# Second stage in 6 chunks of 384 tokens instead of 8 of 288, and the two attention products of a unit issued together

## The chip, the cores and the metric

The kernel runs on one core of a Trainium2 chip. The time is the device time of one execution in microseconds (us). Engines are named as in the profile: PE is TensorE (PEld its weight loads), DVE is VectorE, ACT is ScalarE, POOL is GpSimd, SP is SyncE, which issues the DMAs. "Lnnn" is a line of the kernel before.

## The reference

Inputs are q, k, v of shape (4, 8, 576, 64): batch, heads, sequence, head dimension. Three layers follow each other.

```python
# 1 attention, per head: a pooled one over means of 4 positions, and a local one
out_d = softmax(q_d @ k_d.T / 8) @ v_d          # 144 x 144, repeated 4 times along the sequence
out_local = softmax(where(abs(i - j) < 4, q @ k.T / 8, -1e9)) @ v
x = (repeat(out_d, 4) + out_local)              # to (4, 576, 512)
# 2 channel MLP on the layer norm
x = x + maximum(layernorm(x) * g_ln @ w_ch1, 0) @ w_ch2        # 512 -> 2048 -> 512
# 3 second MLP on mixes of each token with the one ahead of it
xk = mu_k * x + (1 - mu_k) * x_prev ; xr = mu_r * x + (1 - mu_r) * x_prev
k = maximum(xk @ w_k, 0)                                       # 512 -> 1024
out = sigmoid(xr @ w_r) * (k * k @ w_v)                        # 1024 -> 512
```

## The kernel before

All activations lie with the features on the partitions and the tokens along the row. The 2304 tokens are cut into 8 chunks of 288 (N, half a sequence). Weights come as float64 and are turned into float32 by ACT and DVE, then into a high and a low float32r part; a product of two float32 matrices is three float32r matmuls (`mm3`, L192 to L194): high by high, high by low, low by high.

**First stage** (the loop over `seq`): for each chunk c and each f of 16 hidden blocks, `emit_l1` multiplies the normed chunk with a block of the first weight (12 matmuls of 128x288 into h_ps), `emit_l2` multiplies the block's result with the second weight (12 matmuls into four accumulators acc). Between them run the attention and the layer norm of the next chunk, written as generators. A `slot` comes after every six large matmuls; it feeds a budget of DVE time to the generators, and a generator that yields GAP stops until the next feed. So GAP puts at least one feed, six large matmuls, between two steps. `emit_x2` adds the result to x and writes it to memory (x2d, one tensor per chunk); its last token is also copied to edge.

**A unit** of the attention (`unit`) is one chunk and one pair of heads: 8 x 4 units. Its products on PE are the scores (L269 in windows of 30 keys, L273 pooled), four transposes (L316, tile tp), the windowed weights by v (L325, six products) and the pooled weights by the pooled values vd (L333, four products). L325 and L333 write parts of the same tile av; tp and av share one bank of PSUM. Plain float32 products are issued as two matmuls each in the trace, so L325 counts 12 and L333 counts 8 per unit there. Between L325 and L333 stands a GAP:

```python
        yield GAP
        for t in range(2):
            for h in range(2):
                nc.tensor.matmul(
                    av[64 * h:64 * h + 64, N:N + QD],
                    vd[:, t, 64 * h:64 * h + 64], PdT[:, 2 * h + t, :],
```

**Second stage** (the loop over c behind the comment "phase B"): per chunk 8 groups of 12 matmuls with w_k, 4 groups of 12 with w_r and 4 groups of 24 with w_v, 240 in all, each group into one of eight banks (b_ps). `mix` makes xk and xr of a chunk on ACT and DVE, from x2in, which `load_x2` fetches from x2d two chunks ahead; the token ahead of the chunk comes from edge. `start_b`, during the last chunk of the first stage, closes the pools of the attention, opens those of the second stage, and starts `load_b` (the weights, tile wf) and the first mix. Program order on each engine is set by the tile framework's scheduler, which moves an instruction ahead where its inputs and its buffer are ready.

Of the kernel before, what the change touches and what calls it, by code (L numbers as in the profile page):

```python
# [22 lines left out]
N = S // 2  # L23
# [6 lines left out]
NK = DK // 128  # L30


@with_exitstack
def tile_block(ctx: ExitStack, tc: tile.TileContext, qT, kT, vw, vr, vec, mask, w1, w2, wk, wv, wr, out):
# [17 lines left out]
    mask_t = const.tile([128, 2, 3, WIN], F32, name="mask_t")  # L52
    edge = const.tile([128, NCH, KT, 1], F32, name="edge")
    x2d = [dram.tile([128, KT, N], F32, name=f"x2d{c}") for c in range(NCH)]
# [5 lines left out]
    pln = actx.enter_context(tc.tile_pool(name="pln", bufs=1))  # L60

# [142 lines left out]
    PTs = [const.tile([128, 6, 4, 24], F32, name=f"PT{i}") for i in range(2)]  # L204
    kz = [const.tile([128, 2, S + 6], F32, name=f"kz{i}") for i in range(2)]
    kdz = [const.tile([128, 2, SD], F32, name=f"kdz{i}") for i in range(NHP)]
    Ps = [const.tile([128, 6, 32], F32, name=f"P{i}") for i in range(2)]
# [26 lines left out]
    def unit(c, hp, nxt):  # L234
# [95 lines left out]
        yield GAP  # L330
# [32 lines left out]
    def over_features(ps, a, parts):  # L363
        """the mean over the 128 partitions, on all of them"""
# [148 lines left out]
    def emit_x2(c):  # L513
# [6 lines left out]
        nc.gpsimd.tensor_copy(edge[:, c], x[:, :, N - 1:N])  # L520
        nc.sync.dma_start(x2d[c], x)
# [64 lines left out]
    # phase A  # L586
# [29 lines left out]
    def start_b():  # L616
# [3 lines left out]
        xk.extend(bp.tile([128, KT, N], F32R, name=f"xk{i}") for i in range(2))  # L620
# [3 lines left out]
    def load_x2(c):  # L624
        t = xp.tile([128, KT, N + 1], F32, tag="x", name="x2in")
        nc.sync.dma_start(t[:, :, 1:N + 1], x2d[c])
        if c % 2 == 0:
            nc.gpsimd.memset(t[:, :, 0:1], 0.0)
        else:
            nc.gpsimd.tensor_copy(t[:, :, 0:1], edge[:, c - 1])  # L630
        x2in[c] = t

    def mix(c, which):
# [3 lines left out]
        for k in range(KT + 1):  # L637
            if k > 0:
                nc.scalar.copy(dh[:, k - 1, :], prev)
            if k < KT:  # L640
                a = late["bp"].tile([128, N], F32, tag="mixa", name="mixa", bufs=3)
                nc.scalar.activation(a, t[:, k, 1:N + 1], AF.Copy, scale=vec_t[:, 1 + which, k:k + 1])  # L642
# [3 lines left out]
            if k < KT:  # L646
                nc.vector.scalar_tensor_tensor(a, t[:, k, 0:N], omu[:, which, k:k + 1], a, op0=ALU.mult, op1=ALU.add)
# [27 lines left out]
    # phase B  # L675
    bp = late["bp"]
    k2 = [[wpool.tile([128, 4, N], F32R, tag="w", name="k2") for _ in range(2)] for _ in range(2)]
    xr.extend(wpool.tile([128, KT, N], F32R, tag="w", name="xr") for _ in range(2))
# [16 lines left out]
    for c in range(NCH):  # L695
        for f in range(NK):
# [6 lines left out]
            nc.scalar.activation(r, ps[:, 0:N], AF.Relu)  # L703
            nc.vector.tensor_tensor(r, r, ps[:, 0:N], op=ALU.mult)
# [6 lines left out]
        nxt = Feeder(mix(c + 1, 0)) if c + 1 < NCH else Feeder(iter(()))  # L711
        rs = []
        for o in range(KT):
# [3 lines left out]
            for k in range(KT):  # L717
                mm3(ps[:, 0:N], wh[:, k, s], wl[:, k, s], xr[0][:, k, :], xr[1][:, k, :], k == 0, k == KT - 1)
            e = bp.tile([128, N], F32, tag=f"e{o}", name="e")
            nc.vector.tensor_scalar(e, ps[:, 0:N], -87.0, None, op0=ALU.max)  # L720
# [5 lines left out]
        for o in range(KT):  # L726
            ps = bank()
            s = slice(128 * o, 128 * o + 128)
            for f in range(NK):
                (wh, wl), (kh, kl), i = WV[f // 4], k2[f // 4], f % 4  # L730
                mm3(ps[:, 0:N], wh[:, i, s], wl[:, i, s], kh[:, i, :], kl[:, i, :], f == 0, f == NK - 1)
            nxt.feed(2.0)
            ot = bp.tile([128, N], F32, tag="ot", name="ot", bufs=2)
            nc.vector.tensor_tensor(ot, rs[o], ps[:, 0:N], op=ALU.mult)
            nc.sync.dma_start(out[128 * o:128 * o + 128, N * c:N * c + N], ot)
        nxt.drain()
        if c + 1 < NCH:
            pending = Feeder(mix(c + 1, 1))
        if c + 2 < NCH:
# [71 lines left out]
```

## Time and profile before

| | |
|---|---|
| runs | 813.71, 812.79, 815.49 us; median 813.71 us |
| profiled execution | span 812.2 us from the first to the last instruction; the page has no other time of it |
| busy share of the span | PE 95%, PEld 90%, DVE 68%, ACT 51%, POOL 10% |
| instructions | PE 6630, DVE 1330, ACT 1067, POOL 133 |
| moved by DMA | 76.12 MB, 94 GB/s over the span |
| granted PE clock | 0.985 of full speed over the span |

The share of PE is an average over a start in which weights are converted, the first stage and the second stage. A matmul's entry in the timeline is longer than the distance to the next start, because matmuls overlap in the array; the distance of two starts is what a matmul costs. Entries of equal instructions that follow each other closely stand in one row with their count (x12).

### The profile page before, as it was taken

The numbers are of one execution on the slowest core, as the hardware profiler recorded it, in microseconds if no ns is written. First come the engines' busy times: TensorE is split into PE (matmuls) and PEld (weight loads), VectorE is DVE, ScalarE is ACT, GpSimd is POOL, SyncE is SP. The second block draws the span as 40 slices with busy tenths as digits, with TensorE's granted clock in tenths as the row PEclk, the third lists the DMA queues.
The fourth block names the chain that finished last, engine by engine and source line by source line (L and its number), as shares of the span: only waits on it lengthen the run. The fifth ranks groups of instructions, "written<-read, shape, count | busy, mean of one in ns | idle before, by whom it ended". The sixth has DMA issues, their size and how long they took to land.

```text
span 812.2 us, 16778 instructions
## 1 busy us (share of the span) xinstructions
PE 771.0 (95%) x6630; PEld 734.9 (90%) x6630; DVE 554.7 (68%) x1330; ACT 410.7 (51%) x1067; POOL 78.7 (10%) x133
## 2 busy tenths in 40 slices
PE   2559989999999999999999999999999999999998
PEld 1349979999999999999999999999999999999998
DVE  5989987656656645665756545736886976967855
ACT  4889965544544543543554543735454453453440
POOL 3210331001122001122001001001000000000000
PEclk9859999999999999999999999999999999999999
DMA  7797542332342331442332210522202101010000
GB/s 208 232 316 236 152 141 80 110 100 81 98 148 90 104 102 53 115 150 76 100 110 78 91 55 9 158 74 89 59 1 60 51 9 59 20 40 31 8 23 30
DMA packets 39182, 76.12 MB, mean 94 GB/s; under 512 B 4672, under 2 KB 23232, under 8 KB 39104
## 3 DMA queue, kind: packets, MB, share of 16 engines
q1 hardware_dynamic: 39104, 75.06, 29.3%
q8 instruction: 52, 0.85, 0.5%
q14 instruction: 26, 0.21, 0.1%
HBM read 60.36 MB, written 14.68 MB: 92 GB/s over the span
## 4 chain that ended last, share of the span: by engine, by line
PE 90%; DVE 5%; ACT 2%; DMA 2%; issue 1%; SPq 0%; ACTq 0%
PE b_ps L192 10%; PE b_ps L193 10%; PE b_ps L194 10%; PE h_ps L192 9%; PE acc L192 9%; PE h_ps L193 8%; PE acc L194 8%; PE acc L193 8%; PE h_ps L194 8%; PE sc L273 2%; PE av L325 2%; PE sc L269 2%; DMA raw<-in_w 1%; PE av L333 1%; DVE raw L77 1%; PE tp L316 1%
## 5 line engine op out<-in xcount | busy, mean ns | idle before, releaser
L499 DVE SCALAR_TENSOR_TENSOR hl<-h_ps,hh 128x288 fp32r<-128x288 f32 x128 | 58.0, 454 | 86.8 <-ACT hh L498 86.1
L498 ACT ACTIVATE hh<-h_ps 128x288 fp32r<-128x288 f32 x128 | 51.8, 405 | 78.1 <-PE h_ps L194 77.6
L192 PE MATMUL b_ps<-k,wbh 128*128 128x288 f32 x256 | 75.8, 296 | 0.0
L193 PE MATMUL b_ps<-xk,wbh 128*128 128x288 f32 x256 | 75.5, 295 | 0.0
L193 PE MATMUL b_ps<-k,wbh 128*128 128x288 f32 x256 | 75.5, 295 | 0.0
L194 PE MATMUL b_ps<-xk,wbl 128*128 128x288 f32 x256 | 75.5, 295 | 0.0
L194 PE MATMUL b_ps<-k,wbl 128*128 128x288 f32 x256 | 75.3, 294 | 0.0
L192 PE MATMUL b_ps<-xk,wbh 128*128 128x288 f32 x256 | 75.1, 293 | 0.0
L723 DVE RECIPROCAL e<-e 128x288 f32<-128x288 f32 x32 | 62.1, 1944 | 0.1
L305 ACT COPY PT<-T 32x144 f32<-32x144 f32 x128 | 39.5, 309 | 29.7 <-DVE T L301 28.4
L519 POOL TENSOR_TENSOR x<-x2t,x 128x288 f32<-128x288 f32 x32 | 25.0, 813 | 300.5 <-DVE x2t L518 300.5
L642 ACT ACTIVATE mixa<-x2in,vec_t 128x288 f32<-128x288 f32 x64 | 31.6, 530 | 38.3 <-DVE xr L645 36.0
L194 PEld LDWEIGHTS b_ps<-k,wbl 128*128 128x128 f32 x256 | 48.2, 188 | 0.0
L192 PEld LDWEIGHTS b_ps<-xk,wbh 128*128 128x128 f32 x256 | 48.1, 188 | 0.0
L193 PEld LDWEIGHTS b_ps<-xk,wbh 128*128 128x128 f32 x256 | 48.1, 188 | 0.0
L194 PEld LDWEIGHTS b_ps<-xk,wbl 128*128 128x128 f32 x256 | 48.1, 188 | 0.0
L193 PEld LDWEIGHTS b_ps<-k,wbh 128*128 128x128 f32 x256 | 48.1, 188 | 0.0
L192 PEld LDWEIGHTS b_ps<-k,wbh 128*128 128x128 f32 x256 | 48.0, 187 | 0.0
L77 DVE SCALAR_TENSOR_TENSOR raw<-rm 128x512 uint32<-128x512 uint32 x52 | 37.0, 715 | 13.1 <-ACT rm L76 12.7
L693 DVE TENSOR_TENSOR k<-kr,k 128x288 fp32r<-128x288 f32 x64 | 29.2, 457 | 23.6 <-ACT k L692 23.5
L703 ACT ACTIVATE kr<-b_ps 128x288 f32<-128x288 f32 x64 | 26.2, 410 | 36.2 <-PE b_ps L194 36.1
L76 ACT ACTIVATE rm<-raw 128x512 uint8<-128x512 uint8 x52 | 39.9, 784 | 7.7 <-DVE rm L73 7.2
(162 smaller groups left out, 2608.4 us busy)
## 6 DMA issues: line engine op xcount, KB each, us to landing
raw<-in_w SPq DMA_DIRECT2D x32, 512.0 KB
v<-in_vw SPq DMA_DIRECT2D x32, 192.0 KB
bd<-raw SPq DMA_DIRECT2D x20, 256.0 KB
wf<-bd SPq DMA_DIRECT2D x10, 512.0 KB
q<-in_qT SPq DMA_DIRECT2D x32, 148.0 KB
kz<-in_kT SPq DMA_DIRECT2D x32, 145.5 KB
r<-in_vr SPq DMA_DIRECT2D x32, 144.0 KB
x2d<-x SPq DMA_DIRECT2D x8, 576.0 KB
```

What stands on the lines that cost most here:

```text
L76: nc.scalar.activation(low, top, AF.Copy, scale=1.0 / 32.0, bias=-31.0 / 64.0)
L77: nc.vector.scalar_tensor_tensor(raw[:, 0:512].bitcast(U32), ru, 3, m, op0=ALU.logical_shift_left, op1=ALU.bitwise_or)
L192: nc.tensor.matmul(ps, wh, ah, start=first, stop=False)
L193: nc.tensor.matmul(ps, wh, al, start=False, stop=False)
L194: nc.tensor.matmul(ps, wl, ah, start=False, stop=last)
L305: nc.scalar.copy(PT[p, :, j, :], T[p, :, 0:24])
L498: nc.scalar.activation(hh, ps[:, 0:N], AF.Relu)
L499: nc.vector.scalar_tensor_tensor(hl, ps[:, 0:N], 0.0, hh.bitcast(F32), op0=ALU.max, op1=ALU.subtract)
L642: nc.scalar.activation(a, t[:, k, 1:N + 1], AF.Copy, scale=vec_t[:, 1 + which, k:k + 1])
L693: nc.vector.tensor_tensor(l, r, h.bitcast(F32), op=ALU.subtract)
L703: nc.scalar.activation(r, ps[:, 0:N], AF.Relu)
L723: nc.vector.reciprocal(e, e)
```

## The change

Four things are edited.

1. The second stage handles 6 chunks of NB = 384 tokens: its tiles, its matmuls (384 columns) and its element-wise operations are that wide. A chunk is two segments of 192 tokens (SEG), so that a sequence of 576 begins only where a segment does.
2. x2d is one tensor for all tokens. `load_x2` fetches each segment with the token ahead of it, 193 tokens per row, from x2d itself; where a sequence begins it clears that token and fetches 192. The edge tile and its copies are gone. x2in has two buffers of its own in the pool bp, where it used the slots of x.
3. The GAP between L325 and L333 of a unit is gone.
4. PTs, kz, kdz, Ps and mask_t move from the pool const to a pool that is closed with the attention.

```diff
+SEG = 192
+NB = 2 * SEG
+NCB = B * S // NB
...
-    edge = const.tile([128, NCH, KT, 1], F32, name="edge")
-    x2d = [dram.tile([128, KT, N], F32, name=f"x2d{c}") for c in range(NCH)]
+    x2d = dram.tile([128, KT, B * S], F32, name="x2d")
...
                     v[:, n, h, :], PT[:, 3 * h + n, :, :],
                     start=True, stop=True,
                 )
-        yield GAP
         for t in range(2):
...
-        nc.gpsimd.tensor_copy(edge[:, c], x[:, :, N - 1:N])
-        nc.sync.dma_start(x2d[c], x)
+        nc.sync.dma_start(x2d[:, :, N * c:N * c + N], x)
...
     def load_x2(c):
-        t = xp.tile([128, KT, N + 1], F32, tag="x", name="x2in")
-        nc.sync.dma_start(t[:, :, 1:N + 1], x2d[c])
-        if c % 2 == 0:
-            nc.gpsimd.memset(t[:, :, 0:1], 0.0)
-        else:
-            nc.gpsimd.tensor_copy(t[:, :, 0:1], edge[:, c - 1])
+        t = late["bp"].tile([128, KT, 2, SEG + 1], F32, tag="x2in", name="x2in", bufs=2)
+        for i in range(2):
+            n0 = NB * c + SEG * i
+            if n0 % S:
+                nc.sync.dma_start(t[:, :, i, :], x2d[:, :, n0 - 1:n0 + SEG])
+            else:
+                nc.gpsimd.memset(t[:, :, i, 0:1], 0.0)
+                nc.sync.dma_start(t[:, :, i, 1:SEG + 1], x2d[:, :, n0:n0 + SEG])
         x2in[c] = t
...
-                a = late["bp"].tile([128, N], F32, tag="mixa", name="mixa", bufs=3)
-                nc.scalar.activation(a, t[:, k, 1:N + 1], AF.Copy, scale=vec_t[:, 1 + which, k:k + 1])
+                a = late["bp"].tile([128, NB], F32, tag="mixa", name="mixa", bufs=3)
+                a2 = a.rearrange("p (i n) -> p i n", i=2)
+                nc.scalar.activation(a2, t[:, k, :, 1:SEG + 1], AF.Copy, scale=vec_t[:, 1 + which, k:k + 1])
...
-    for c in range(NCH):
+    for c in range(NCB):
         for f in range(NK):
...
-                mm3(ps[:, 0:N], wh[:, k, o:o + 128], wl[:, k, o:o + 128], xk[0][:, k, :], xk[1][:, k, :], k == 0, k == KT - 1)
-            r = bp.tile([128, N], F32, tag="kr", name="kr", bufs=3)
+                mm3(ps[:, 0:NB], wh[:, k, o:o + 128], wl[:, k, o:o + 128], xk[0][:, k, :], xk[1][:, k, :], k == 0, k == KT - 1)
+            r = bp.tile([128, NB], F32, tag="kr", name="kr", bufs=3)
```

In the changed file the lines stand a little lower: L325 is L328 there, L333 is L335, the matmuls of `mm3` are L195 to L197. In the rows that follow, `av` is the output of a unit's products, `PT` and `PdT` are the transposed weights, `h_ps` and `acc` belong to the first stage's large matmuls.

PE in the first stage, around the two products of a unit; before:

```order
L194 MATMUL acc<-hh,w_1l 128x288
L325 MATMUL av<-PT_109,v 64x96 x6
L192 MATMUL h_ps<-ah,w_1h 128x288
L193 MATMUL h_ps<-al,w_1h 128x288
L194 MATMUL h_ps<-ah,w_1l 128x288
...
L333 MATMUL av<-PdT,vd 64x72 x4
```

and in the changed kernel:

```order
L197 MATMUL acc<-hh,w_1l 128x288
L328 MATMUL av<-PT_104,v 64x96 x6
L335 MATMUL av<-PdT,vd 64x72 x4
L195 MATMUL h_ps<-ah,w_1h 128x288
L196 MATMUL h_ps<-al,w_1h 128x288
L197 MATMUL h_ps<-ah,w_1l 128x288
```

Before, six large matmuls stand between the two products; now none does. Over the whole program 27 units stand as in the first piece and one as in the second before; after the change all 28 units that run beside the large matmuls stand as in the second (the four units of the first chunk run ahead of them).

SP's queue, where the second stage begins (wf are the weights that are loaded again, out the results); before:

```order
L521 DMA x2d_94<-x 128x1152
L626 DMA x2in<-x2d_88 128x4x288
L176 DMA wf<-bd 128x1024 x7
L521 DMA x2d_95<-x 128x1152
L626 DMA x2in<-x2d_89 128x4x288
L626 DMA x2in<-x2d_90 128x4x288
L735 DMA out<-ot 128x288 x2
```

and in the changed kernel:

```order
L522 DMA x2d<-x 512x1x288
L634 DMA x2in<-x2d 128x4x192
L631 DMA x2in<-x2d 128x4x193
L179 DMA wf<-bd 128x1024 x2
L631 DMA x2in<-x2d 128x4x193
L179 DMA wf<-bd 128x1024
L634 DMA x2in<-x2d 128x4x192
L179 DMA wf<-bd 128x1024 x4
L522 DMA x2d<-x 512x1x288
L631 DMA x2in<-x2d 128x4x193 x2
L740 DMA out<-ot 128x384 x2
```

Each load of x2in is now two DMAs, and the load for the second chunk stands between the reloads of the weights, ahead of the last x2d write, where it stood behind that write.

## Rows read from the trace of the kernel before

**Rows 1.** Page, first line: the span.
```profile
span 812.2 us, 16778 instructions
```

**Rows 2.** Windows: start:end us, then busy us (x instructions) of each engine, PEclk, DMA share, GB/s.
```profile
0.00:59.80 59.80, 25.43 (x229) 18.02 (x229) 46.71 (x115) 40.90 (x98) 15.88 (x37) 0.80 0.80 251
59.80:140.00 80.20, 77.18 (x694) 70.95 (x694) 71.77 (x176) 61.81 (x148) 17.87 (x22) 1.00 0.50 155
140.00:540.00 400.00, 400.00 (x3693) 377.88 (x3693) 238.83 (x659) 192.77 (x542) 40.02 (x62) 1.00 0.31 97
553.20:808.40 255.20, 255.20 (x1921) 254.99 (x1920) 193.54 (x374) 113.55 (x277) 4.43 (x12) 1.00 0.12 38
553.20:585.10 31.90, 31.90 (x242) 31.90 (x242) 27.36 (x57) 17.18 (x44) 3.49 (x8) 1.00 0.21 67
```

**Rows 3.** Timeline of PE, one unit: start us, length us, engine, line, operation.
```profile
208.63 0.29 PE L194 MATMUL acc<-hh,w_1l 128*128 128x288 f32 x1
208.86 0.72 PE L325 MATMUL av<-PT,v 128*64 128x96 f32 x12
...
209.88 0.29 PE L194 MATMUL h_ps<-ah,w_1l 128*128 128x288 f32 x1
...
210.27 0.29 PE L194 MATMUL h_ps<-ah,w_1l 128*128 128x288 f32 x1
210.49 0.47 PE L333 MATMUL av<-PdT,vd 72*64 72x72 f32 x8
...
211.27 0.29 PE L194 MATMUL h_ps<-ah,w_1l 128*128 128x288 f32 x1
```

**Rows 4.** Timeline of PE, a unit with both products as neighbours; left out: two large matmuls.
```profile
112.30 0.29 PE L193 MATMUL acc<-hl,w_3h 128*128 128x288 f32 x1
112.52 0.72 PE L325 MATMUL av<-PT,v 128*64 128x96 f32 x12
113.07 0.42 PE L333 MATMUL av<-PdT,vd 72*64 72x72 f32 x8
...
113.78 0.29 PE L192 MATMUL acc<-hh,w_3h 128*128 128x288 f32 x1
```

**Rows 5.** Lines, PE, 140 to 540 us: busy us, mean ns.
```profile
L325 PE MATMUL av<-PT,v 128*64 128x96 f32 x288 | 17.2, 255 | 0.0
```

**Rows 6.** Tile vd: ns min/median/max, first and last start.
```profile
L231 POOL TENSOR_TENSOR vd<-r x32: 449/460/812, 15.1 to 368.0; 72x128 f32<-72x128 f32 x32
```

**Rows 7.** Timeline of PE: six plain float32 products in a row.
```profile
63.08 1.62 PE L420 MATMUL var<-xc,ones 128*128 128x288 f32 x6
```

**Rows 8.** Tile var, the same products: ns min/median/max.
```profile
L420 PE MATMUL var<-xc,ones x8: 403/406/406, 59.4 to 64.3; 128*128 128x288 f32 x8
```

**Rows 9.** Windows: a stretch at the lower clock, and two of the second stage.
```profile
55.10:57.98 2.88, 2.88 (x14) 2.88 (x14) 2.71 (x6) 2.03 (x4) 0.00 (x0) 0.50 1.02 408
730.00:740.00 10.00, 10.00 (x77) 10.00 (x77) 10.00 (x14) 2.43 (x7) 0.00 (x0) 1.00 0.06 20
740.00:750.00 10.00, 10.00 (x77) 10.00 (x77) 5.58 (x14) 4.20 (x11) 0.00 (x0) 1.00 0.12 43
```

**Rows 10.** Timeline of PE in the stretch at the lower clock.
```profile
56.01 0.44 PE L192 MATMUL h_ps<-ah,w_0h 128*128 128x288 f32 x1
56.25 0.44 PE L194 MATMUL h_ps<-ah,w_0l 128*128 128x288 f32 x1
```

**Rows 11.** Tile x2in: what its engines waited for (us, times).
```profile
  DMA x2in<-x2d: 1.5, 2
```

**Rows 12.** Timeline, all engines, the end of the kernel.
```profile
808.46 0.45 DVE L734 TENSOR_TENSOR ot<-e,b_ps 128x288 f32<-128x288 f32 x1 [2.75 <-PE b_ps L194]
808.94 0.33 SPq L735 DMA_DIRECT2D out<-ot  x1
```

**Rows 13.** Timeline of PE: a transpose behind a large matmul.
```profile
94.87 0.29 PE L194 MATMUL acc<-hh,w_2l 128*128 128x288 f32 x1
95.00 0.41 PE L316 MATMUL tp<-ident,Pd 72*72 72x72 f32 x4
```

More of the change, by code (lines that the diff above doesn't have):

```diff
@@ L51, in tile_block @@
     ident = const.tile([QD, QD], F32, name="ident")
-    mask_t = const.tile([128, 2, 3, WIN], F32, name="mask_t")
-    edge = const.tile([128, NCH, KT, 1], F32, name="edge")
-    x2d = [dram.tile([128, KT, N], F32, name=f"x2d{c}") for c in range(NCH)]
+    x2d = dram.tile([128, KT, B * S], F32, name="x2d")
     actx = ExitStack()
@@ L60, in tile_block @@
     pln = actx.enter_context(tc.tile_pool(name="pln", bufs=1))
+    pone = actx.enter_context(tc.tile_pool(name="pone", bufs=1))
+    mask_t = pone.tile([128, 2, 3, WIN], F32, name="mask_t")
     def in_order(on, ins):
@@ L203, in tile_block @@
     av_user = []
[L204 to L207, printed above, removed]
+    PTs = [pone.tile([128, 6, 4, 24], F32, name=f"PT{i}") for i in range(2)]
+    kz = [pone.tile([128, 2, S + 6], F32, name=f"kz{i}") for i in range(2)]
+    kdz = [pone.tile([128, 2, SD], F32, name=f"kdz{i}") for i in range(NHP)]
+    Ps = [pone.tile([128, 6, 32], F32, name=f"P{i}") for i in range(2)]
     def load_qk(c, hp):
@@ L619, in start_b @@
         late["bp"] = bp = ctx.enter_context(tc.tile_pool(name="bp", bufs=1))
-        xk.extend(bp.tile([128, KT, N], F32R, name=f"xk{i}") for i in range(2))
+        xk.extend(bp.tile([128, KT, NB], F32R, name=f"xk{i}") for i in range(2))
         late["parts"] = [load_b(), mix(0, 0)]
@@ L646, in mix @@
             if k < KT:
-                nc.vector.scalar_tensor_tensor(a, t[:, k, 0:N], omu[:, which, k:k + 1], a, op0=ALU.mult, op1=ALU.add)
+                nc.vector.scalar_tensor_tensor(a2, t[:, k, :, 0:SEG], omu[:, which, k:k + 1], a2, op0=ALU.mult, op1=ALU.add)
                 prev = a
@@ L676, in tile_block @@
     bp = late["bp"]
-    k2 = [[wpool.tile([128, 4, N], F32R, tag="w", name="k2") for _ in range(2)] for _ in range(2)]
-    xr.extend(wpool.tile([128, KT, N], F32R, tag="w", name="xr") for _ in range(2))
+    k2 = [[wpool.tile([128, 4, NB], F32R, tag="w", name="k2") for _ in range(2)] for _ in range(2)]
+    xr.extend(wpool.tile([128, KT, NB], F32R, tag="w", name="xr") for _ in range(2))
     ring = [(ps_h, "h"), (ps_h, "h"), (ps_at, "sc"), (ps_at, "av")] + [(ps_acc, f"acc{o}") for o in range(KT)]
@@ L710, in tile_block @@
         pending.drain()
-        nxt = Feeder(mix(c + 1, 0)) if c + 1 < NCH else Feeder(iter(()))
+        nxt = Feeder(mix(c + 1, 0)) if c + 1 < NCB else Feeder(iter(()))
         rs = []
@@ L717, in tile_block @@
             for k in range(KT):
-                mm3(ps[:, 0:N], wh[:, k, s], wl[:, k, s], xr[0][:, k, :], xr[1][:, k, :], k == 0, k == KT - 1)
-            e = bp.tile([128, N], F32, tag=f"e{o}", name="e")
-            nc.vector.tensor_scalar(e, ps[:, 0:N], -87.0, None, op0=ALU.max)
+                mm3(ps[:, 0:NB], wh[:, k, s], wl[:, k, s], xr[0][:, k, :], xr[1][:, k, :], k == 0, k == KT - 1)
+            e = bp.tile([128, NB], F32, tag=f"e{o}", name="e")
+            nc.vector.tensor_scalar(e, ps[:, 0:NB], -87.0, None, op0=ALU.max)
             nc.scalar.activation(e, e, AF.Exp, scale=-1.0)
@@ L730, in tile_block @@
                 (wh, wl), (kh, kl), i = WV[f // 4], k2[f // 4], f % 4
-                mm3(ps[:, 0:N], wh[:, i, s], wl[:, i, s], kh[:, i, :], kl[:, i, :], f == 0, f == NK - 1)
+                mm3(ps[:, 0:NB], wh[:, i, s], wl[:, i, s], kh[:, i, :], kl[:, i, :], f == 0, f == NK - 1)
             nxt.feed(2.0)
-            ot = bp.tile([128, N], F32, tag="ot", name="ot", bufs=2)
-            nc.vector.tensor_tensor(ot, rs[o], ps[:, 0:N], op=ALU.mult)
-            nc.sync.dma_start(out[128 * o:128 * o + 128, N * c:N * c + N], ot)
+            ot = bp.tile([128, NB], F32, tag="ot", name="ot", bufs=2)
+            nc.vector.tensor_tensor(ot, rs[o], ps[:, 0:NB], op=ALU.mult)
+            nc.sync.dma_start(out[128 * o:128 * o + 128, NB * c:NB * c + NB], ot)
         nxt.drain()
-        if c + 1 < NCH:
+        if c + 1 < NCB:
             pending = Feeder(mix(c + 1, 1))
-        if c + 2 < NCH:
+        if c + 2 < NCB:
             load_x2(c + 2)
```

4 lines of the change are left out of this document (2 added, 2 removed).

## The prediction

> **What bounds the kernel now.** The page gives a span of 812.2 us [rows 1], and its busy table names TensorE (PE) as the busiest engine. That is an average, so I read the busy times by stretch next [rows 2]: up to 59.8 us PE is busy 25.43 us only and VectorE (DVE) sets the pace; from 59.8 to 140 us PE lacks 3.0 of 80.2 us; from 140 to 540 us it is busy all 400 us; in the second stage (553.20 to 808.40 us) it is busy all 255.20 us, beside a DVE with 27.36 us of work in a chunk of 31.90 us. So from 140 us on, only what PE itself does can make the kernel shorter or longer, and I read the timeline of PE next. The reader should see two things in it. A matmul of 288 columns starts every 0.13 us, and around each product of the attention the distance is longer than the product needs. The span is 1.5 us below the 813.71 us median of the runs (812.79 to 815.49); the page has no other time of that execution, so I add the differences to the median.
>
> **The two products of a unit.** In a unit of the attention the windowed product (L325) and the pooled one (L333) now stand 1.6 us apart with six large matmuls between them [rows 3]. From the last large matmul ahead of the first product to the third one behind it go 209.88 - 208.63 = 1.25 us; for the second product 211.27 - 210.27 = 1.00 us. Without a product those three steps take 3 x 0.133 = 0.40 us (0.133 is 255.20 us over 1921 matmuls, [rows 2]). So the products cost 0.85 + 0.60 = 1.45 us apart. One unit of the trace has them side by side already [rows 4]: 113.78 - 112.30 = 1.48 us, less 0.40, is 1.08 us. Side by side saves 0.37 us by rows with two decimals, so 0.35 to 0.39; I take 0.36. What goes is one change from 128-column to 64-column products and back, which PE does not overlap.
>
> The order of the changed kernel puts all 28 units beside the large matmuls in this form; of before 27 are split. The 288 products of L325 from 140 to 540 us [rows 5] are 24 units of 12, where PE never waits: 24 x 0.36 = **8.6 us** off. The other three split units lie before 140 us, where the DVE and the weight conversion set the pace in part: I take nothing, the bound is another 3 x 0.36 = 1.1 us. The later product comes one feed earlier, about 1 us. It can't wait longer for its ScalarE (ACT) input: the first product writes the bank that this copy reads, so it has waited for the copy already. Its GpSimd input vd is early: the last of the 32 additions that make it starts at 368.0 us [rows 6], in the chunk before the two that read it. Behind it on PE stand only the large matmuls. The first 59.8 us keep their order but for a few neighbours on DVE and ACT: nothing, with 1 us either way for the range.
>
> **The matmuls of the second stage.** Before: 8 chunks of 240 matmuls with 288 columns, 1920 at 132.8 ns, 255.0 us. After: 6 x 240 = 1440 with 384 columns; the columns in all stay the same. At the full clock of 2.4 GHz 288 columns are 120.0 ns, so a matmul has 12.8 ns more than its columns. Is that a cost per matmul or per column? The trace has this kind of matmul (float32r) with 288 columns alone, so I bound it.
> - Nearest row: the six plain float32 products of L420, also 288 columns and 128 weights wide, take 1.62 us from the first start to the last end [rows 7], one lasts 406 ns [rows 8], so they start (1.62 - 0.406)/5 = 242.8 ns apart, against 240.0 for 288 columns at two cycles each: 2.8 ns fixed.
> - At half the clock (granted 0.50, that is 1.2 GHz, [rows 9]) the float32r matmul starts every 0.24 us [rows 10]: 288 columns at 1.2 GHz and nothing more. The excess does not double with the slower clock, it vanishes. So something that runs beside the array is exposed at full speed only: a start of each row of data, or a limit on columns per second.
> - If it is fixed, 160.0 + 12.8 = 172.8 ns, 1440 of them 248.8 us: 6.2 us less. If it all goes by columns, 177.1 ns and 255.0 us: nothing.
>
> I take the fixed cost, **6.2 us** off: the half-clock row shows the array to be the only limit there, and 12.8 ns as a rate would be 2.17 columns per ns, close to the array's own 2.4 without a reason in the rows for the odd ratio. Both ends stay for the range.
>
> By the Trainium skill (TensorE: Matmul & The Clock Gate, "Back-to-back issue gap") a warm matmul takes N/2.4 + 2.5 ns, which is 122.5 ns here where the trace has 132.8. By that rule the 480 saved matmuls are worth 480 x 2.5 = 1.2 us (an estimate from that page), so it speaks against this part of the change; its fixed part agrees with the 2.8 ns of the float32 rows.
>
> **Everything around them.** DVE and ACT handle the same elements in fewer, longer instructions: at most 27.36 x 4/3 = 36.5 us of DVE in a chunk of 240 x 172.8 ns = 41.5 us, so PE still covers it. The reloading of x2 becomes 12 pieces instead of 8 transfers, in rows of 192 or 193 words instead of 288. Now ACT waited 1.5 us in all for these loads [rows 11] and PE not at all; the load still goes out a chunk ahead, and its tiles no longer wait for the slots of x: nothing. The written x2 goes out as 512 rows instead of 128; its reader comes a chunk or more later: nothing. The edge copies leave GpSimd, which is off the path; on its queue two of the four clears of x2in now stand ahead of the last four additions of L519, and clear tiles that nobody held. On SP's queue the load for the second chunk now stands ahead of five weight reloads, and waits for nothing recent. Moving small tiles to another pool issues nothing.
>
> The tail grows. The last DVE multiply takes 0.45 us, its DMA goes out at 808.94 and the span ends at 812.2 [rows 1, 12]. The multiply gets 0.15 us longer at most, the last matmul 0.04, and a DMA of 192 instead of 144 KB between nothing and a third of 3.3 us: I take +0.4, bounds 0 and 1.3.
>
> Sum: -8.6 - 6.2 + 0.4 = -14.4 us; 813.7 - 14.4 = **799.3 us** (span 797.8). With the unit saving of 0.35 to 0.39, the three early units and the first stretch, this case reaches from about 797 to 801.5.
>
> **Rivals.**
> 1. The excess goes by columns. All of it: -8.6 + 0.0 + 0.4, 805.5 us. With 2.8 ns fixed and 10.0 ns by columns: 2.8 + 130.0 x 4/3 = 176.1 ns, 253.6 us, -1.4 us, 804.1 us. For it: the float32 rows have 2.8 ns fixed only. Against: nothing in the rows runs at 2.17 columns per ns otherwise. The Trainium skill's rule named above is of this kind.
> 2. The matmuls wait for their weights: 132.8 ns would be a weight load, and 384 columns would hide it. Then 160 + 2.8 = 162.8 ns, 234.4 us, -20.6 us: 784.9 us. Against: a transpose with 72 weight columns instead of 128 also starts 0.13 us behind the large matmul ahead of it [rows 13]; the shorter load buys nothing.
> 3. Slower: longer rows of data lose more, because the reads of PE share the memory with the other engines and fall behind. From 182.8 ns per matmul on (255.0 + 8.6 - 0.4 = 263.2 us over 1440) the kernel is no faster. Were the excess to double, 160 + 25.6 = 185.6 ns, 267.3 us: +12.3 - 8.6 + 0.4, 817.8 us. Against: PE issues 77 matmuls in 10 us beside a DVE busy 10.00 us as beside one busy 5.58 us [rows 9].
> 4. The saving in the first stage is eaten by another engine there: -6.2 + 0.4, 807.9 us. Against: DVE is busy 238.83 of 400 us there [rows 2].
>
> **How the numbers follow.** Forecast 0.66; rival 1 0.22; rival 2 0.05; rival 3 0.04; rival 4 0.03. The range from 797.0 to 806.5 holds the forecast's case nearly whole and rival 1, less the tails that I can't name: about 0.8. A measurement of this kernel can tell 0.3%, 2.4 us, from no change. The first two and rivals 2 and 4 are faster by more than that, 0.96; I keep 0.92 for them, because the first 140 us may shift by more than I allow, 0.03 for no change and 0.05 for slower, rival 3 and the like.
>
> **What would show it.** In the profile after, the products of L328 and L335 stand in one row behind the other with about 1.08 us per pair, and the stretch that was 400 us is 8 to 9 us shorter; PE is busy throughout from 140 us on. In the second stage the matmuls start 0.17 us apart: 172.8 ns if the forecast is right, 176 to 177 in rival 1, 163 in rival 2, 183 or more in rival 3, each over 1440 of them. DVE's share of a chunk falls. The prediction is wrong if PE shows idle time after 140 us, if a pair side by side costs 1.45 us as before, or if the first 140 us move by more than 2 us.

## The result and the profile after

The changed kernel takes **803.03 us** (median; 801.98 to 803.84), a ratio of 0.9869 to the kernel before, 95% interval 0.9851 to 0.9887. Of 813.7 us that is 10.7 us less (9.2 to 12.1). The forecast was 799.3 us with a range of 797.0 to 806.5: the sign and the range held, the gain came out 3.7 us smaller than the sum of 14.4. (A fourth run of the kernel before, 814.70 us, puts its median at 814.21; what follows stays with the 813.7 on which the forecast is built.)

The page after, its first lines and groups of matmuls of the second stage (columns of a group: busy us, mean ns of one, idle us ahead):

```profile
span 799.9 us, 15611 instructions
...
PE 758.2 (95%) x6150; PEld 731.3 (91%) x6150; DVE 546.4 (68%) x1234; ACT 398.7 (50%) x995; POOL 76.6 (10%) x121
...
L197 PE MATMUL b_ps<-xk,wbl 128*128 128x384 f32 x192 | 64.9, 338 | 0.0
...
L197 PE MATMUL b_ps<-k,wbl 128*128 128x384 f32 x192 | 64.1, 334 | 0.0
```

The span was 812.2 us [rows 1]. Two things are to be seen. PE has no idle time ahead of these matmuls. And the two groups, the same instruction with the same 384 columns, differ: those that read xk last 338 ns, those that read k 334.

The windows by stage, after (start:end, length, then busy us of each engine, PEclk, DMA share, GB/s):

```profile
0.00:59.80 59.80, 25.53 (x233) 18.67 (x234) 47.56 (x117) 41.37 (x100) 16.35 (x37) 1.00 0.81 258
59.80:140.00 80.20, 77.10 (x701) 72.93 (x700) 73.58 (x180) 63.08 (x151) 19.01 (x21) 0.98 0.48 153
140.00:530.00 390.00, 388.97 (x3666) 373.52 (x3665) 236.08 (x650) 188.61 (x534) 37.97 (x57) 1.00 0.33 102
540.00:796.00 256.00, 256.00 (x1480) 256.00 (x1480) 184.86 (x282) 102.22 (x207) 3.30 (x6) 1.00 0.10 33
```

Against [rows 2]: the first 59.8 us are the same in PE's busy time (25.43 us before, 25.53 after), though the granted clock over them was 0.80 before and 1.00 after; in the second stage PE is busy throughout, and in the long stretch of the first stage 1.03 us are missing of 390. They are new; before, PE was busy all of the 400 us there. The view of what PE waited for, after, from 60 us on (in total, times, longest):

```profile
PE tp L319 <- ACT Pd L295: 2.4, 1, 2.4
PE acc L195 <- ACT hh L500: 1.0, 1, 1.0
PE h_ps L196 <- DVE al L397: 0.6, 1, 0.6
```

A unit of the attention in the timeline of PE, after (start, length, engine, line, operation):

```profile
205.85 0.29 PE L197 MATMUL acc<-hh,w_1l 128*128 128x288 f32 x1
206.06 0.72 PE L328 MATMUL av<-PT,v 128*64 128x96 f32 x12
206.61 0.42 PE L335 MATMUL av<-PdT,vd 72*64 72x72 f32 x8
206.96 0.40 PE L195 MATMUL h_ps<-ah,w_1h 128*128 128x288 f32 x1
207.20 0.30 PE L196 MATMUL h_ps<-al,w_1h 128*128 128x288 f32 x1
207.33 0.29 PE L197 MATMUL h_ps<-ah,w_1l 128*128 128x288 f32 x1
```

The pair stands side by side as in [rows 4], and from the last large matmul ahead to the third behind go 207.33 - 205.85 = 1.48 us, the number of that row.

In what follows the *first stage* is the time from the first matmul into h_ps to the last into acc, the *second* from there to the last into b_ps, both from the starts in the trace's records. Of the 12.3 us between the two profiled spans, 0.4 lie ahead of the first stage (53.85 to 53.42 us), 6.95 in the first (499.19 to 492.24), 4.50 in the second (255.09 to 250.59) and 0.4 behind (4.08 to 3.67). The sum had 0, 8.6, 6.2 and -0.4 there.

These cuts are rough in two ways. After the change the second stage's first three matmuls run ahead of the last ones into acc, so the first stage holds 0.5 us of the second's work. And the first chunk, beside which the weights are converted, lasts between 71.1 and 74.5 us in the profiles of all runs in the table below but e8, whatever the change, while everything behind it repeats to a few hundredths of a us in kernels with the same order and places. So that table has two stretches without the first chunk: chunks 2 to 7 of the first stage, and chunk 8 with the second stage (a chunk ends where its last matmul into acc starts). The change took 7.36 us off the one, where the step on the products had 8.6, and 2.55 off the other, where the step on the second stage had 6.2.

### The profile page after: what moved, and what is told of

It reads as the page before. It is cut to its first block, busy times and chain, and to the rows that moved or that the text cites. A ratio compares the mean times of both kernels' runs of the same rounds, so it can differ in the third digit from the quotient of the medians.

```text
span 799.9 us, 15611 instructions
## 1 busy us (share of the span) xinstructions
PE 758.2 (95%) x6150; PEld 731.3 (91%) x6150; DVE 546.4 (68%) x1234; ACT 398.7 (50%) x995; POOL 76.6 (10%) x121
## 4 chain that ended last, share of the span: by engine, by line
PE 83%; DVE 7%; DMA 5%; ACT 4%; issue 1%; SPq 0%; ACTq 0%
PE b_ps L196 10%; PE b_ps L195 10%; PE b_ps L197 10%; PE h_ps L195 8%; PE acc L195 7%; PE acc L196 7%; PE acc L197 7%; PE h_ps L196 7%; PE h_ps L197 7%; DMA raw<-in_w 4%; PE av L328 2%; PE sc L276 2%; PE sc L272 2%; DVE raw L80 1%; PE tp L319 1%; PE av L335 1%
## 5 line engine op out<-in xcount | busy, mean ns | idle before, releaser
L197 PE MATMUL b_ps<-xk,wbl 128*128 128x384 f32 x192 | 64.9, 338 | 0.0
L195 PE MATMUL b_ps<-xk,wbh 128*128 128x384 f32 x192 | 64.9, 338 | 0.0
L196 PE MATMUL b_ps<-xk,wbh 128*128 128x384 f32 x192 | 64.8, 338 | 0.0
L197 PE MATMUL b_ps<-k,wbl 128*128 128x384 f32 x192 | 64.1, 334 | 0.0
L195 PE MATMUL b_ps<-k,wbh 128*128 128x384 f32 x192 | 64.1, 334 | 0.0
L196 PE MATMUL b_ps<-k,wbh 128*128 128x384 f32 x192 | 64.1, 334 | 0.0
L728 DVE RECIPROCAL e<-e 128x384 f32<-128x384 f32 x24 | 61.1, 2544 | 0.1
L647 ACT ACTIVATE mixa<-x2in,vec_t 128x384 f32<-128x384 f32 x48 | 28.1, 613 | 37.3 <-DVE xr L650 34.8
L195 PE MATMUL acc<-hh,w_1h 128*128 128x288 f32 x128 | 40.4, 319 | 1.0 <-ACT hh L500 1.0
L195 PE MATMUL h_ps<-ah,w_0h 128*128 128x288 f32 x128 | 39.4, 309 | 1.2 <-ACT ah L394 1.2
L195 PE MATMUL h_ps<-ah,w_2h 128*128 128x288 f32 x128 | 40.0, 312 | 0.0
L195 PE MATMUL acc<-hh,w_2h 128*128 128x288 f32 x128 | 39.9, 315 | 0.0
```

The source lines that it names most:

```text
L195: nc.tensor.matmul(ps, wh, ah, start=first, stop=False)
L196: nc.tensor.matmul(ps, wh, al, start=False, stop=False)
L197: nc.tensor.matmul(ps, wl, ah, start=False, stop=last)
L647: nc.scalar.activation(a2, t[:, k, :, 1:SEG + 1], AF.Copy, scale=vec_t[:, 1 + which, k:k + 1])
L728: nc.vector.reciprocal(e, e)
```

## The experiments

The runs in one table, times in us; "rows of xk" is the mean distance from the start of a matmul that reads xk to the next start, over all 576 (before: 768, of 288 columns), "of k" the same for k. Each ratio goes with the kernel before on the same chip.

| run | median | ratio, 95% interval | chunks 2 to 7 | chunk 8 and second stage | rows of xk, ns | of k, ns |
|---|---|---|---|---|---|---|
| before | 813.71 | | 375.42 | 304.93 | 132.26 | 133.33 |
| after | 803.03 | 0.9869 (0.9851 to 0.9887) | 368.06 | 302.38 | 176.12 | 173.33 |
| e1_join_only | 805.08 | 0.9894 (0.9880 to 0.9909) | 367.28 | 304.94 | as before | as before |
| e2_chunks_only | 810.27 | 0.9965 (0.9953 to 0.9978) | 375.96 | 302.24 | as after | as after |
| e3_split_three | 820.73 | 1.0093 (1.0078 to 1.0109) | 384.81 | 302.23 | as after | as after |
| e4_xk_shift | 801.50 | 0.9857 (0.9844 to 0.9871) | 368.05 | 300.91 | 173.42 | 173.33 |
| e6_all_shift32 | 802.50 | 0.9872 (0.9851 to 0.9892) | 368.05 | 302.35 | 176.14 | 173.33 |
| e7_x2_held | 801.24 | 0.9856 (0.9835 to 0.9878) | 368.05 | 300.91 | as e4 | as e4 |
| e8_sync | 808.86 | 0.9944 (0.9925 to 0.9962) | 378.90 | 301.04 | as e4 | as e4 |
| e9_mix_late | 799.93 | 0.9835 (0.9819 to 0.9852) | 368.05 | 299.45 | 173.35 | 173.33 |
| e10_places | 801.41 | 0.9858 (0.9835 to 0.9882) | 367.52 | 300.97 | 173.37 | 173.33 |
| e11_late_places | 799.47 | 0.9832 (0.9817 to 0.9847) | 367.53 | 299.47 | 173.29 | 173.33 |
| e12_late_all224 | 800.08 | 0.9843 (0.9827 to 0.9859) | 368.06 | 300.76 | 173.35 | 173.33 |

Differences of a few tenths of a us can be read from the two stretches; the ratios can't tell them apart.

**One half of the change at a time.** e1 is the kernel before without the line that parts the two products; e2 is the changed kernel with that line put back.

```diff
 # e1, from the kernel before
-        yield GAP
 # e2, from the kernel after
+        yield GAP
```

> The kernel before with one edit: no GAP between the windowed and the pooled product of a unit; second stage as before, 8 chunks of 288. Theory (each split costs a change of PE from 128-column to 64-column products and back, 0.35 us): 24 units beside a busy PE gain 24 x 0.35 = 8.4 us, so about 805.8 against 814.2, and the stretch from 140 us to the first second-stage matmul is 8 us shorter. Rival (the saving in the first stage is eaten by another engine, and the gain of the change comes from its second stage): 812 or more.

> The changed kernel with the GAP put back: 6 chunks of 384 and split products. Theory (a fixed 13 to 16 ns per matmul, 480 matmuls fewer): the second stage lasts 251 us instead of 255, so about 810 against 814.2. Rival (cost by column): 814. The two experiments together should give the sum of the change, 11 us.

Measured: e1 0.9894, which is 8.6 us less (7.4 to 9.8) of the 813.13 us that the kernel before took beside it; e2 0.9965, 2.8 us less (1.8 to 3.8). The join is worth what the step said, 8.6. The wider chunks are worth half of their 6.2 - 0.4 = 5.8 us; most of what is missing is missing there. In chunks 2 to 7, beside which 24 units run, e1 takes 8.14 us less than before, 0.34 us for a unit. In the unit itself, over all units of the traces, the products cost 0.85 and 0.60 us apart and 1.10 side by side: 0.35 saved, 27 units 9.5 us.

**The price of one more interruption.** If a change from 128-column products to 64-column ones and back costs 0.35 us wherever it stands, splitting each unit in three instead of one must cost twice that per unit.

```diff
 # e3, from the kernel after: in the loop over n of L328, and behind it
+            if n == 2:
+                yield GAP
...
+        yield GAP
```

> The changed kernel with two GAPs: one inside the windowed product (two of its three windows, then the third) and one ahead of the pooled product, so a unit's products stand in three places instead of one. Its order has 146 places where other products stand between the large matmuls, the changed kernel 90. Theory (0.35 us per change): 56 x 0.35 = 19.6 us, less what falls into the first 140 us, so 803.0 + 17 to 20 = 820 to 823. Rival (the saving came from a wait that went, not from the change of columns): 803 to 814.

Measured 1.0093, 820.73 us. The order has 146 places where other products stand between the large matmuls, 120 in e2, 90 in the kernel after. From e2 to e3 that is 26 more at 0.35 us, 9.1 us, and 10.5 us were measured; from after to e3 56 more, 19.6 us, against 17.7. In chunks 2 to 7 alone e3 takes 16.75 us more than the kernel after, for 48 more places of its 24 units, 0.35 us each, while PE stands idle there for no more than 0.1 us. So the price of a place of these products holds in both directions, and it isn't a wait.

**Why the matmuls that read xk are slower.** The timeline of PE in the second stage of the kernel after, the first and the last of 24 matmuls on xk, then of 24 on xr:

```profile
599.80 0.34 PE L195 MATMUL b_ps<-xk,wbh 128*128 128x384 f32 x1
...
603.84 0.34 PE L197 MATMUL b_ps<-xk,wbl 128*128 128x384 f32 x1
604.02 0.33 PE L195 MATMUL b_ps<-xr,wbh 128*128 128x384 f32 x1
...
608.01 0.33 PE L197 MATMUL b_ps<-xr,wbl 128*128 128x384 f32 x1
```

The 23 steps take 4.04 us for xk and 3.99 for xr, 175.7 and 173.5 ns by rows with two decimals; over all of them it is 176.12 and 173.32. The second number is 160 ns of columns and 13.33 fixed, and the matmuls on k had 133.33 before, 120 and 13.33, on each of the tile's four rows. The first is the number of rival 1 (176.1). What sets xk apart is where it lies: by the addresses in the built program its tiles begin 128 bytes behind a multiple of 256, those of xr, k and the weights on one. e4 puts 128 bytes ahead of xk.

```diff
 # e4, from the kernel after
-        xk.extend(bp.tile([128, KT, NB], F32R, name=f"xk{i}") for i in range(2))
+        t0 = bp.tile([128, 32 + KT * NB], F32R, name="xk0")
+        xk.append(t0[:, 32:32 + KT * NB].rearrange("p (k n) -> p k n", k=KT))
+        xk.append(bp.tile([128, KT, NB], F32R, name="xk1"))
```

> The changed kernel with xk's first tile 128 bytes longer at its front, so that both xk tiles begin 128 bytes further in the memory; nothing else moves but what lies behind them. In the changed kernel the matmuls that read xk start 176.0 ns apart, those that read xr and k 173.3 ns. Theory A (where a row begins in the memory decides those 2.7 ns): xk comes to 173.3 ns, 576 x 2.7 = 1.5 us less, 801.5. Theory B (it is what stands beside these matmuls, the work of ACT and DVE in that part of a chunk): 176.0 ns as before and 803.0.

Measured: 173.42 ns, and chunk 8 with the second stage 300.91 us, 1.47 less. The page of e4, the same two groups:

```profile
L197 PE MATMUL b_ps<-xk,wbl 128*128 128x384 f32 x192 | 64.1, 334 | 0.0
L197 PE MATMUL b_ps<-k,wbl 128*128 128x384 f32 x192 | 64.1, 334 | 0.0
```

e6 shifts everything by 32 bytes, the weights too (8 more words in the tile vec_t, which lies ahead of all of them): xk at 160, xr, k and the weights at 32.

```diff
-    vec_t = const.tile([128, 3, KT], F32, name="vec_t")
+    vec_t = const.tile([128, 3 * KT + 8], F32, name="vec_t")[:, 0:3 * KT].rearrange("p (w k) -> p w k", w=3)
```

> The changed kernel with 32 bytes more in the first small tile, so that every later tile begins 32 bytes further. The rows of ah, al, hh and hl then begin at the same places modulo 256 bytes as in the kernel before (32 or 160), xk at 160, xr and k at 32. Theory (the place of a row decides a few ns): the matmuls of the first stage that read ah and al go from 132.9 and 133.4 ns back to 132.1 to 132.4 ns, 1536 of them, about 1 us less in the first stage; xk, xr and k move off 176.1 and 173.3 ns by 1 to 3 ns. Rival (places do not matter beyond xk): all as in the changed kernel, 803.

Measured 176.14 and 173.33 ns, as in the kernel after. So neither the place of xk by itself (160 is as bad as 128) nor that of the weights (32 is as good as 0) decides; in both kernels the distance between the two is 128 bytes modulo 256.

**Fixed cost, or a weight load?** Narrow matmuls tell the forecast from rival 2: SEG = 96 makes 12 chunks of 192 columns.

```diff
-SEG = 192
+SEG = 96
```

> The changed kernel with segments of 96, so the second stage goes in 12 chunks of 192 tokens, 2880 matmuls. A fixed cost alone (13.3 ns as in xr and k with 288 and with 384 columns) gives 80.0 + 13.3 = 93.3 ns per matmul. A cost by column gives 89 ns (192 x 133.3/288). A weight load that 192 columns can no longer cover gives more than both: 110 ns, the distance of two weight loads behind a transpose, or up to 133 ns.

Measured: 873.55 us in a single run beside 812.79, and 111.65 ns per matmul on xk and xr, 111.8 on k. That is neither 80 + 13.3 = 93.3 nor 80 + 2.8. Its timeline, PE and the weight loads (PEld):

```profile
599.78 0.28 PE L195 MATMUL b_ps<-xk,wbh 128*128 128x192 f32 x1
599.80 0.19 PEld L196 LDWEIGHTS b_ps<-xk,wbh 128*128 128x128 f32 x1
599.89 0.28 PE L196 MATMUL b_ps<-xk,wbh 128*128 128x192 f32 x1
599.92 0.19 PEld L197 LDWEIGHTS b_ps<-xk,wbl 128*128 128x128 f32 x1
600.01 0.28 PE L197 MATMUL b_ps<-xk,wbl 128*128 128x192 f32 x1
```

Loads and matmuls follow each other in one beat of 0.11 us that the columns no longer fill: the most likely reading is that here the weight load sets it. Then it needs 111.65 ns, less than the 133.33 of 288 columns: at 288 columns it was covered already, against rival 2. It fits that xk, which lies 128 bytes off here too, costs no more than xr. The issuing of load and matmul isn't what sets it: the twelve products of L325, each with a load of its own, start within 0.55 us [rows 4]. By the Trainium skill (TensorE: Matmul & The Clock Gate, "LDWEIGHTS (loading the stationary operand)") a load of P columns takes P/1.2 ns, 106.7 for 128 (an estimate from that page); the beat measured here is 5 ns longer.

**The new wait for hh.** The timeline of ACT in the kernel after, then of PE:

```profile
505.62 0.41 ACT L500 ACTIVATE hh<-h_ps 128x288 fp32r<-128x288 f32 x1 [0.85 <-PE h_ps L197]
508.22 0.62 ACT L647 ACTIVATE mixa<-x2in,vec_t 128x384 f32<-128x384 f32 x1 [2.19 <-DMA x2in<-x2d]
...
516.85 2.16 ACT L83 CAST wbh<-wf 128x512 fp32r<-128x512 f32 x4
518.92 0.69 ACT L500 ACTIVATE hh<-h_ps 128x288 fp32r<-128x288 f32 x2
```

```profile
518.05 0.29 PE L197 MATMUL h_ps<-ah,w_2l 128*128 128x288 f32 x1
519.37 0.80 PE L195 MATMUL acc<-hh,w_1h 128*128 128x288 f32 x4 [1.03 <-ACT hh L500]
```

ACT stands 2.19 us before the first scaling of the reloaded x2 (before: 0.27), runs late with all that follows, and at 519.37 PE waits 1.03 us. What SP waited for ahead of the load, after, then before (in total, times, longest):

```profile
SPq L634 <- DVE y L438: 5.2, 1, 5.2
```

```profile
SPq L626 <- DMA x2d<-x: 2.4, 1, 2.4
```

Before, x2in took a slot of x, and the load went out at 509.25 us, 2.5 us ahead of the layer norm's last step (y, at 511.79). Now x2in stands in the pool bp, which opens on the memory of the attention's pools, and the load waits for that step: y starts at 502.48 and ends at 502.94, and the load goes out at 503.07. From there to the scaling pass 5.10 us before and 5.15 after (509.25 to 514.35, 503.07 to 508.22), so the load takes no longer, it starts later. It comes with the wider chunks: PE has no wait for hh in e1, and one of 0.9 us in e2.

In 506.0 to 508.3 us, while the load is under way, the DMA engines are busy all the time and move 360 GB/s. Two theories on what to mend: the load of the second chunk of x2, which goes out beside it, slows it (e7 holds that one back, on top of e4); or the scaling stands too early in ACT's queue for a load that starts so late (e9 pins it behind four more evacuations, also on top of e4).

```diff
 # e7, both loads of L631 and L634
-                nc.sync.dma_start(t[:, :, i, :], x2d[:, :, n0 - 1:n0 + SEG])
+                in_order(c == 1, nc.sync.dma_start(t[:, :, i, :], x2d[:, :, n0 - 1:n0 + SEG]))
 # e9
-            if n >= 20 and n % 4 == 0:
+            if n >= 24 and n % 4 == 0:
...
-                nc.scalar.activation(a2, t[:, k, :, 1:SEG + 1], AF.Copy, scale=vec_t[:, 1 + which, k:k + 1])
+                in_order(c == 0 and which == 0 and k == 0, nc.scalar.activation(a2, t[:, k, :, 1:SEG + 1], AF.Copy, scale=vec_t[:, 1 + which, k:k + 1]))
```

> E4's kernel (xk shifted) with the load for the second chunk of the second stage kept behind the weight reloads and the last x2d write on SP's queue, as in the kernel before. Theory (the early load shares the DMA engines with the first chunk's load; ACT waits 2.3 us for that one with the evacuation of a large matmul behind it, and PE 1.1 us): ACT's wait falls under 1 us, PE's wait goes, 1 us less than E4's 801.5, so 800.5. Rival (the first load is late by itself, or by the weight reloads beside it): the waits stay and 801.5.

> The kernel with the first product's rows shifted (e4), and the first scaling of the second stage's input (L645's a2, first of chunk 0) pinned behind four more of the first stage's evacuations on ScalarE. Theory: in the kernel after, ScalarE waits 2.2 us there for the reloaded x2, the evacuation hh behind it comes late, and TensorE waits 1.0 us for it. Pinned later the load has landed, TensorE's wait of 1.0 to 1.1 us for hh is gone, and the time is 1.0 us below e4: 800.5 us, ratio about 0.9845 of before. Rival: the evacuation is late for another reason (the weight conversions ahead of it on ScalarE), then the wait stays 1.0 to 1.4 us and the time is that of e4, 801.5 us. Second rival: the scaling itself is now what the second stage's first product waits for, and 1 us or more shows as a wait on b_ps instead.

e7: PE still waits 1.1 us for hh; the second load isn't the cause. e9: the wait is gone. What PE waited for in e9 from 60 us on:

```profile
PE tp L319 <- ACT Pd L295: 2.2, 1, 2.2
PE acc L196 <- DVE hl L501: 0.7, 1, 0.7
```

and ACT's timeline there, where the scaling (now L649) starts 12 us later and waits for nothing:

```profile
519.76 0.62 ACT L83 CAST wbh<-wf 128x512 fp32r<-128x512 f32 x1 [1.19 <-PE acc L196]
520.29 0.61 ACT L649 ACTIVATE mixa<-x2in,vec_t 128x384 f32<-128x384 f32 x1
```

The ratio is 0.9835, where e4 had 0.9857; the intervals overlap, but chunk 8 and the second stage are 1.46 us shorter than in e4 (300.91 to 299.45): the wait cost that much, somewhat more than the 1.1 us for which PE stood. Whether the reloads of weights, which run beside the load of x2, slow it was not tried.

**Fewer column changes still.** If 0.35 us is the price of a place, standing the scores beside the products of the unit ahead should save more. e8 lets the scores of a unit go out only when the products of the one ahead of it have.

```diff
 # e8, on top of e4
+    av_out = set()
...
+        while hp > 0 and (c, hp - 1) not in av_out:
+            yield GAP
...
+        av_out.add((c, hp))
```

> E4's kernel with the scores of a unit held until the unit ahead of it has issued its two products, so that they stand side by side on PE: 79 places with other products between the large matmuls instead of 90, and 20 units have scores beside products. Theory (0.35 us per change of columns, so here 20 x 0.35 = 7 us less for scores that no longer stand alone, less transposes that now stand alone again, under 0.1 us each): 801.5 - 6 = 795. Rival (the later scores make the units late and PE waits at the end of a chunk): 801 or more.

Measured 0.9944, slower than e4 by 7 us, with 79 places instead of 90. PE's waits in e8:

```profile
PE av L331 <- ACT PdT L325: 6.2, 5, 1.7
PE acc L195 <- ACT hh L504: 1.2, 1, 1.2
PE h_ps L195 <- ACT ah L398: 1.2, 1, 1.2
```

The units now come late for ACT, and PE waits 6.2 us for PdT; all its waits from 60 us on come to 10.9 us, in e4 to 4.1. The saving is smaller than expected, too: a place with a unit's products and the next one's scores costs 1.99 us, and 1.09 and 1.08 us when they stand apart, so 0.18 is saved and not 0.35. Twenty such places are 3.6 us at best; the waits cost more. The 0.35 us is the price of a place of the two products, not of any place: four transposes cost 0.30 us where they stand alone, of which their own starts, 61 to 66 ns apart, take 0.25. The gap between scores and products is cover, and the one within the pair of products was not.

**The places of the first stage's tiles.** In the kernel after the matmuls into h_ps start 132.86 ns apart (those on ah) and 133.35 (on al), before 132.18 and 132.33 (means of the distance to the next start, over those under 0.2 us). The mask and other small tiles left the first pool, and with that the weights' tiles went from 224 bytes modulo 256 to 0 and ah, al from 32 to 0. (A row of 288 words is 1152 bytes, so the rows of ah and al lie in turn at the place named and 128 bytes further.) e10 puts them back (on top of e4), e11 is e10 with the scaling of e9, e12 is e9 with every tile at 224.

```diff
 # e10 and e11; e12 without the two lines on gap
-    vec_t = const.tile([128, 3, KT], F32, name="vec_t")
+    vec_t = const.tile([128, 3 * KT + 56], F32, name="vec_t")[:, 0:3 * KT].rearrange("p (w k) -> p w k", w=3)
...
+    gap_pool = ctx.enter_context(tc.tile_pool(name="gapp", bufs=1))
     xp = ctx.enter_context(tc.tile_pool(name="xp", bufs=2))
...
+    nc.gpsimd.memset(gap_pool.tile([128, 16], F32, name="gap"), 0.0)
```

> The kernel e4's layout with the weights' tiles and the tiles ah and al put back to the places they had in the kernel before (224 and 32 bytes modulo 256; 0 and 0 in the kernel after); xk's first tile comes to 160 and its second to 32. Theory: the h_ps matmuls of the first stage went from 132.35 to 132.85-133.4 ns because of those places; put back they start 132.1 to 132.4 ns apart, 1536 of them, 0.8 to 1.5 us less in the first stage. Rival: the places of these tiles do nothing, the spacing stays 132.8 and 133.4 ns, and the first stage stays at 492 to 494 us; what is left then is xk's place, 176.1 ns for its 192 rows of one kind if 160 counts like 128 (second stage 250.6 us).

> The pinned scaling of e9 and the tiles' places of e10 in one kernel. If the two savings are independent: TensorE waits for no hh, h_ps matmuls start 132.2 and 132.7 ns apart instead of 132.8 and 133.4 (0.7 ns, 1536 of them: 1.1 us), and the time is 0.8 to 1.1 us below e9 (799.9 us): about 799 us, ratio 0.982 to 0.983. Rival: what the h_ps matmuls save is waited for elsewhere in the first stage, and the time is that of e9.

> As e11, but every tile of the large matmuls stands at 224 modulo 256 bytes, the weights and ah, al, xk and xr alike; the order of all engines is that of e9. It tells which place the h_ps matmuls feel. If it is the weights' own (224 instead of 0), they start 132.2 and 132.7 ns apart as in e10 and e11; if it is that of the rows ah and al (32 in before, e10 and e11; 0 in after), or the distance between the two, they stay at 132.8 and 133.4 or slower. xk's and xr's rows at 224: 173.3 ns if only places near 128 are bad, up to 176.1 if 224 counts as 128 and 160 do.

| run | weights at | ah, al at | h_ps on ah, ns | on al, ns | xk at | rows of xk, ns |
|---|---|---|---|---|---|---|
| after | 0 | 0 | 132.86 | 133.35 | 128 | 176.12 |
| e6 | 32 | 32 | 132.83 | 133.33 | 160 | 176.14 |
| e9 | 0 | 0 | 132.79 | 133.48 | 0 | 173.35 |
| e12 | 224 | 224 | 132.83 | 133.52 | 224 | 173.35 |
| e10 | 224 | 32 | 132.18 | 132.73 | 32 | 173.37 |
| e11 | 224 | 32 | 132.22 | 132.66 | 32 | 173.29 |

The expectation of e10 gave xk two places, 160 and 32; since the rows still begin 128 bytes into its first tile, both stand at 32. The table answers: with weights and rows at the same place modulo 256, whichever it is, the h_ps matmuls take 132.8 and 133.3 to 133.5; with the rows 64 bytes further, 0.6 to 0.9 ns less. It is the distance again. The time shows it where it can be read so finely: in chunks 2 to 7 e10 and e11 take 0.53 us less than e4 and e9, and e12 takes what those take. In the whole it is lost: e10 has the ratio of e4 (0.9858 and 0.9857), the median of e11 is 0.5 and 0.6 us below those of e9 and e12, inside their intervals, and in its first chunk e11 waits 1.2 us for xsum, which e9 does not. e12 waits 0.8 us for hh and hl in chunk 8, which e9 does not; why stays open.

**The best version** is e9 or e11, which a measurement can't tell apart: 799.93 and 799.47 us, ratios of 0.9835 and 0.9832. The interval of e11 ends at 0.9847, below that of the change alone, which begins at 0.9851.

## Why the prediction was right, and where it was not

**The bound.** Right: from 140 us on only PE's own work counted, and the one new wait of 1.03 us stood in the time at once, with nothing to hide it. PE's idle time after 140 us was also one of the prediction's own signs of being wrong, and it pointed at a step that was wrong (x2in, below).

**The two products.** Right in mechanism and size: 1.48 us for a pair with its neighbours as in [rows 4], 0.35 us saved against 0.36, and 8.6 us in all by e1 against 8.6 (8.1 of them in chunks 2 to 7, where the step had all 8.6). With its interval of 7.4 to 9.8 e1 can't say whether the three early units, which the step put at nothing, gave their 1.1. What is shown is the price of a place of these products. That the change of the column count costs it is not: the transposes change it as well, to 72, and pay little beyond their own starts.

**The matmuls of the second stage.** The fixed cost was right, the size was off. On k the excess is 13.33 ns at 288 columns and at 384, so it is per matmul; the step had 12.8, which is the mean over matmuls of several kinds (132.26 on xk, 133.14 on xr, 133.33 on k before), and 0.5 ns over 1440 matmuls are 0.7 of its 6.2 us. What failed is that it took all matmuls of the stage to be of one kind: the change put xk's rows at a distance where each loses 2.7 ns, 576 of them 1.5 us. With that and the wait for hh mended, chunk 8 and the second stage are 5.48 us shorter than before (e9), about what 1440 matmuls at 173.33 ns leave of 255.1. By the Trainium skill (TensorE: Matmul & The Clock Gate, "Back-to-back issue gap") the isolated gap of a warm matmul with 384 columns is 162.5 ns (an estimate from that page); the trace has 173.33, and the saving that the rule gave, 1.2 us, is a fifth of that 5.48.

**Rival 1** seems to win: its 176.1 ns is what the matmuls on xk show, and the 803.0 us lie nearer to its 804.1 than to the forecast's 799.3. It was chance: the same instruction on other tiles shows 173.33, and a shift by 128 bytes brings xk there. **Rival 2** fell with the result, as it asked for 162.8 ns where 173.33 came, and e5 agrees. **Rival 3** had a grain of truth, longer rows that lose more, but by the tiles' places and not by other engines' traffic, and by 2.7 ns instead of the 10 that it needed. **Rival 4** did not come: nothing ate the 8.6.

**"Nothing" for x2in and for SP's queue.** Wrong by 1.5 us. The step saw that the tiles of x2in "no longer wait for the slots of x", and took them for tiles "that nobody held". But their new pool opens on memory that the attention and the layer norm had: SP's load stands 5.2 us for the layer norm's last step and goes out behind it, where it went out 2.5 us ahead of it before. So ACT waits 2.2 us at the first scaling, and that reaches PE through the evacuation behind it. The step read ACT's small wait before (1.5 us in all, [rows 11]) and PE's none as slack; it should have asked who had the new memory last, and which evacuation stands behind the scaling. e9 shows the cost.

**"Moving small tiles to another pool issues nothing."** True, and still it had an effect: it moved every tile that lies behind them, and the matmuls into h_ps start 0.7 to 1.0 ns further apart. In chunks 2 to 7 that is 0.8 us: the kernel after takes 368.06 us there, and e1, with the same order of PE and the old places, 367.28.

**The tail.** -0.4 us where +0.4 was taken (0 to 1.3). The last multiply grew by 0.11, from 0.45 to 0.56 us as the step had it, but from the issue of the last DMA to the end of the span it is 2.7 us, against 3.3 before [rows 1, 12]. The end of the kernel after, all engines:

```profile
796.25 0.34 PE L197 MATMUL b_ps<-k,wbl 128*128 128x384 f32 x1
796.62 0.56 DVE L739 TENSOR_TENSOR ot<-e,b_ps 128x384 f32<-128x384 f32 x1 [3.61 <-PE b_ps L197]
797.21 0.33 SPq L740 DMA_DIRECT2D out<-ot  x1
```

It isn't noise: e1, with the old chunks, has 3.3 us there as well, and the runs with 384 columns 2.7 to 2.8, all but e8 (3.1). Why less follows behind a larger DMA is not settled.

Together: 14.4 less 0.5 (the products in chunks 2 to 7), 0.8 (h_ps), 0.7 (12.8 for 13.33 ns), 1.5 (xk's place) and 1.5 (hh), plus 0.8 (tail), is 10.2 us, and up to 1.1 more if the three early units gave theirs; 10.7 were measured (9.2 to 12.1). With xk's place and the scaling mended the same sum gives 13.2, and e9 is 13.4 us faster (12.0 to 14.7). That the 14.4 of the forecast lies in that interval is luck in part: the tail's 0.8 stands against 2.0 of the other terms.

## What to carry to other kernels

Where a chain of matmuls is the bound, count the places at which smaller products interrupt it, price each kind of place in the trace, put two of them side by side where their inputs are ready, and stop where that makes one wait for another engine. Fewer and longer matmuls save a fixed cost each; find it by a second column count on the same tiles before it is taken for a rate, and look at the means for each tile that is read, not at the mean over a stage. An edit that only moves or resizes small tiles moves every tile behind them, and a tile in a pool that opens on another's memory waits for that one's last user: a load that was just in time is then just late.

## What the runs showed that was not expected

The distance between the weights and the rows that a float32r matmul reads, modulo 256 bytes, changes its pace. At 384 columns it is 173.3 to 173.4 ns at distances of 0 and 64, and 176.1 at 128. At 288 columns, where the rows of a tile alternate between two distances, h_ps has 132.8 (ah) and 133.4 (al) at 0 and 128, and 132.2 and 132.7 at 64 and 192. There 128 is no worse than 0: k's rows before stand at both in turn, and each takes 133.33. The place itself (0, 32 or 224 for the weights) does nothing. One number does not fit: the matmuls on xr take 173.85 ns in e10 and e11 at distance 0, and 173.33 in all others. Why the distance matters, no run here shows.

With 192 columns a float32r matmul with its 128-column weights starts every 111.65 ns and no sooner, so below some 236 columns ((111.65 - 13.33) x 2.4) nothing is saved by narrower rows, if both readings hold.
